# The sign of a float64 weight by a parametric relu on the scalar engine, and a rebuilt order

## The chip, the cores and the metric

The kernel runs on one core of a Trainium2 chip. A core has five engines that run side by side and wait for each other by semaphores: TensorE (PE in the rows; PEld is its weight load), VectorE (DVE), ScalarE (ACT), GpSimd (POOL) and SyncE (SP), which issues the transfers here. The metric is device time in microseconds (us). Each run is one launch of the whole program.

## The reference, cut to what matters

An attention over packed keys feeds two pairs of layers.

```python
p_packed = sm_attn(p, k, v)                 # 8 batches, 8 heads, 576 keys, 32 packed rows
x = sm_attn(q, p_packed, p_packed)          # 4608 tokens x 512
h = x @ w_in                                # 512 -> 2048
P = a[0] + a[1]*h + a[2]*h**2 + a[3]*h**3
Q = 1.0 + abs(b[0])*abs(h) + abs(b[1])*h**2
x = (P / (Q + 1e-06)) @ w_out               # 2048 -> 512
h = x @ w2_in
out = (h - tanh(h)) @ w2_out                # the second pair, same sizes
```

The four weight matrices (`w_in`, `w_out`, `w2_in`, `w2_out`) arrive as float64, everything else as float32. The kernel reads each float64 as a pair of 32-bit words, and the core itself makes float32 values of them.

## The kernel before, in words

The 4608 tokens are cut into ten column blocks n of 384 or 512 tokens (`XW`). A chunk g = 8 n + p is one block and one of eight pieces p of the 2048 hidden columns. For each chunk PE runs `l1` (L610, 12 products per piece of a block, into a two-deep PSUM ring `h`), ACT, POOL and DVE make the rational function, and PE runs `l2` (L623), 16 products with the high part `gh` and 8 with the low part `gl`, into four accumulators. High and low parts together give float32 products out of a faster format, so each layer has three products for one. Six DVE instructions belong to a chunk: L648 and L652 (`front_2`, `front_3`, which read `h`), then L665, L667, L671 and L674 (`back`); L665 writes `gh`, L674 writes `gl`. POOL has one, L645; ACT has five (L633, L637, L641, L657, L658).

Ahead of a block stand a softmax over the packed rows (L502 to L546, on DVE and ACT; L517, L531 and L546 may go to POOL instead) and, for each batch, the packed attention (scores L398, exponent L414, transposes L428, values L443) and a product of `pp` with the first weight (L475), split into high and low by ACT L484 and DVE L488 into `slot`. So the second matrix of the attention is folded into `w_in`.

The second pair follows the 80 chunks: nine blocks of 512 tokens, in each 16 steps of `l3` (L736, 12 products), tanh (ACT L742), subtraction (DVE L745), split into high (ACT L750) and low (DVE L753) and `l4` (L766 to L768, 12 products).

**Float64 weights.** They come as 33 pieces of up to 1 MB into the tile `raw`, of which there are two (`RAW = 2`); a third piece waits until the first is done with. A piece has two words for each number. The class `Weights` makes float32 of them in place:

- step "1" on DVE: L309 shifts the low word right by 29 bits. L312 then takes the sign bit of the high word (and) and puts it on the low word (or).
- step "A" on ACT: L320 multiplies the high word, read as float32, by 2^-112.
- step "2" on DVE: L325 shifts that left by 3 bits and joins it (or) with the low word.

The planner has these as `d1`, `dA` and `d`, each waiting for the one ahead of it. For the weights of `l2`, `l3` and `l4` there follow ACT L933 (high part) and DVE or POOL L937 (low part); the eight pieces of `l1`'s weight go to `w`, which L475 reads, and are stored back to memory for the later batches. Sixteen pieces (`w1`, `w2`) are needed by the first block, the other 17 by the second pair.

**Order.** The class `Plan` sets each engine's order when the program is built: a list of work with costs, `after` lists and due times; at each turn the engine that can start soonest takes the due-first work among what can start within its `SLACK`. The due times are offsets in the table `DUE`. Each engine then runs its instructions in this order, and one that waits holds all behind it. A work marked `port=True` also keeps POOL and DVE apart: POOL's next work waits for the DVE work that stands ahead of it.

Of the kernel before, what the change touches and what calls it, by code (L numbers as in the profile page):

```python
# [12 lines left out]
AF = mybir.ActivationFunctionType  # L13
ALU = mybir.AluOpType
# [3 lines left out]
LN2 = 0.6931471805599453  # L18


DUE = {"G0": 15.294, "G1": -3.281, "A2": 4.445, "P_W": -1.767, "P_F": -15.98, "P_R": -8.628, "P_B": -2.149, "P_2": 3.709, "P_3": 4.233, "P_E": 4.677, "P_4": 7.085, "D_Y": 1.328, "b0": 3.208, "b1": -2.115, "b2": -0.452, "b3": 0.917, "l2h": 2.411, "l2l": 0.922, "f2": -18.573, "f3": -3.699, "fu": 2.695, "ft": 11.608, "fq": -4.098, "gH": -21.109, "gL": -7.224, "mx": -4.057, "ex": 1.371, "z": -6.028, "et": -3.273, "ta": 2.123, "av": -1.372, "y": 4.265, "bt": -27.441, "bd": 5.818, "si": -12.623, "sx": -14.679, "ss": 8.057, "se": -16.289, "sz": 2.679, "sn": 8.64, "so": 7.528, "sh": 11.803, "sl": 7.641, "w1": 1.591, "w2": -1.036, "w3": 7.691, "wh": 5.275, "wl": 2.512, "x": 5.311, "u2": -4.84, "u3": 7.277, "u4": -3.765, "u5": -4.641, "uu0": -3.053, "uu1": -1.728, "r0": -4.745, "dA": 26.416, "wd": -6.518, "d": 1.166}

SLACK = {"ALT": 0, "DVE": 0, "PE": 0.0, "ACT": 97.8, "POOL": 830.6, "SP": 0}


class Plan:
# [11 lines left out]
    ALT = 600  # L38
# [8 lines left out]
    def add(self, name, engine, cost, run, after=(), due=0.0, take=None, free=(), behind=(), late=None, port=None):  # L47

        assert name not in self.work, name
        port = "POOL" in engine if port is None and engine else port
        self.work[name] = [engine, cost, run, list(after), due, take, list(free), list(behind), late, port]
# [116 lines left out]
def packed_attention_moe_kernel(  # L170
# [27 lines left out]
    act, dve, pool, pe, sp = nc.scalar, nc.vector, nc.gpsimd, nc.tensor, nc.sync  # L198
# [32 lines left out]
    def cut(t, n, c=2):  # L231

        return t[:, 0:c * XW[n]].rearrange("p (c t) -> p c t", c=c)
    G0, G1, A2, P_W, P_F, P_R, P_B, P_2, P_3, P_E, P_4, D_Y = (
        DUE[x] for x in "G0 G1 A2 P_W P_F P_R P_B P_2 P_3 P_E P_4 D_Y".split()
    )

    def O(x):
        return DUE.get(x, 0.0)

# [33 lines left out]
    b0, b1 = cabs[:, 0:1], cabs[:, 1:2]  # L274
# [5 lines left out]
    class Weights:  # L280
# [24 lines left out]
        def step(self, j, step, dst=None):  # L305
            w = self.words(j, U32) if wide else None
            if step == "1":

                dve.tensor_scalar(  # L309
                    out=w[:, :, 0], in0=w[:, :, 0], scalar1=29, scalar2=None, op0=ALU.logical_shift_right  # L310
                )
                dve.scalar_tensor_tensor(  # L312
                    out=w[:, :, 0], in0=w[:, :, 1], scalar=0x80000000, in1=w[:, :, 0],
                    op0=ALU.bitwise_and, op1=ALU.bitwise_or,
                )
            if step == "A":


                f = self.words(j)
                act.activation(out=f[:, :, 1], in_=f[:, :, 1], func=AF.Copy, scale=2.0 ** -112)  # L320
            if step == "2":
                def like(x):
                    return x if dst is None else x.rearrange("p (a f) -> p a f", a=4)

                dve.scalar_tensor_tensor(  # L325
                    out=w[:, :, 0] if dst is None else dst.bitcast(U32),
                    in0=like(w[:, :, 1]), scalar=3, in1=like(w[:, :, 0]),
                    op0=ALU.logical_shift_left, op1=ALU.bitwise_or,
                )
            if step == "copy":  # L330
                pool.tensor_copy(out=dst, in_=self.got[j][0].rearrange("p (a f) -> p a f", a=4))
# [13 lines left out]
    sx = ctx.enter_context(ExitStack())  # L345
# [5 lines left out]
    bd, pp = {}, {}  # L351
# [439 lines left out]
    add = plan.add  # L791

    def c_act(n, pointers=0, sbuf=0):
        return 0.833 * n + 52 + 93 * pointers + 43 * sbuf

    def c_dve(n):
        return 1.04 * n + 70
# [64 lines left out]
    for j, (kind, i) in enumerate(pairs):  # L862
        if kind == "w1":
            srcs = w1_parts(i)
            due, free = i - 3.0 + O("w1"), []
            if i % 2 == 0 and i >= 2 * WB:
                gone = (i - 2 * WB, i - 2 * WB + 1)
                free = [("g", 0, x) for x in gone] + ([("w1d", x) for x in gone] if wide and B > 1 else [])
        else:
            if kind == "w2":  # L870
                srcs, slots_, due, free = [w2[2 * i], w2[2 * i + 1]], w2_slot[2 * i:2 * i + 2], i + 0.8 + O("w2"), []
            elif kind == "w3":
                srcs, slots_, due = [w3[i], w3[i + 1]], w3_slot[i:i + 2], total - 16 + 4 * i + O("w3")
            else:
                srcs, slots_, due = [w4[i]], [(w4_slot, i)], total + i - D_Y
                if i + PRE < NF:
                    srcs.append(w3[i + PRE])
                    slots_.append(w3_slot[i + PRE])
            if kind != "w2":
                free = []  # L880
                for x in slots_:
                    if not isinstance(x, tuple):
                        free += last_use(x)
                    elif x[1] < len(w4_slot):
                        free += last_use(x[0][x[1]])
                    else:
                        free += [("open y",)]

            def slots_now(slots_=slots_):
                return [x[0][x[1]] if isinstance(x, tuple) else x for x in slots_]  # L890

        k = len(srcs)
        w1s = kind == "w1"
        if w1s:
            names = [("w1", 0, i)]
        else:
            names = {"w2": [("w2", 2 * i), ("w2", 2 * i + 1)], "w3": [("w3", i), ("w3", i + 1)],
                     "w43": [("w4", i), ("w3", i + PRE)][:k]}[kind]
        if j == NX:
            add_extra()  # L900
        old = raw_free()
        for c, src in enumerate(srcs):
            dma(("raw", j, c), 512 * 128 * (8 if wide else 4), lambda j=j, c=c, src=src: weights.load(j, c, src),
                old, due - 1.5 + O("r0") * (j < 8), behind=raw_next(("raw", j, c)))
        raw_user.append(list(names))
        loads = [("raw", j, c) for c in range(k)]

        def step(x, j=j, w1s=w1s, i=i):
            if w1s and x in ("2", "copy"):
                if i % 2 == 0:  # L910
                    w1_tile(0, i // 2)
                w1_kept[i] = half(w1_t[0, i // 2], i)
                weights.step(j, x, half(w1_t[0, i // 2], i))
            else:
                weights.step(j, x)

        if wide:
            add(("d1", j), "DVE", 90 + k * 800, lambda f=step: f("1"), loads, due, port=True)
            add(("dA", j), "ACT", c_act(512 * k, 0, 1), lambda f=step: f("A"), [("d1", j)], due + O("dA"))
            add(("d", j), "DVE", c_dve(512 * k), lambda f=step: f("2"), [("dA", j)] + (free if w1s else []), due + O("d"), port=True)  # L920
        elif w1s:
            add(("d", j), "POOL", k * 1900, lambda f=step: f("copy"), loads + free, due)
        else:
            add(("d", j), None, 0, lambda: None, loads, due)
        if w1s:
            plan.alias(("w1", 0, i), ("d", j))
            if wide and B > 1:
                dma(("w1d", i), 128 * 4096, lambda i=i: sp.dma_start(out=half(w1d[i // 2], i), in_=w1_kept.pop(i)), [("d", j)], due + 1 + O("wd"))
        else:
            for c in range(k):  # L930
                def high(c=c, j=j, get=slots_now):
                    h, l = halves(get()[c])
                    act.activation(out=h, in_=weights.pieces(j)[c], func=AF.Copy)  # L933

                def low(by, c=c, j=j, get=slots_now):
                    h, l = halves(get()[c])
                    by.tensor_tensor(out=l, in0=weights.pieces(j)[c], in1=h.bitcast(F32), op=ALU.subtract)  # L937

                add(("wh", j, c), "ACT", c_act(512, 0, 1), high, [("d", j)] + free, due + 0.2 + O("wh"))
                add(names[c], ("POOL", "DVE"), (c_low(512), c_dve(512)), low, [("wh", j, c)], due + 0.3 + O("wl"))  # L940
# [19 lines left out]
    for u in range(2 * B):  # L960
        b, d = u // 2, UNIT(u)
# [32 lines left out]
    for b in range(B):  # L994
        for p in range(NP):
            d = p - 2.0 if b == 0 else blocks_of(b)[0] * NP + p - G0
            i = b * NP + p
            k = 2 if b else 1
            if p % k == 0:
# [6 lines left out]
                for y in range(k):  # L1006
                    if i + y >= NG:
                        x, y = divmod(i + y - NG, NP)
# [196 lines left out]
```

## Time and profile before

| | |
|---|---|
| device time, median of 3 runs | 1639.33 us (1637.66 to 1640.53) |
| profiled execution, device time | 1636.56 us |
| its span, first to last instruction | 1634.6 us |
| mean granted TensorE clock | 0.975 |
| busy: PE, DVE, ACT, POOL | 1550.9, 1032.2, 784.7, 180.9 us |
| instructions: PE, DVE, ACT, POOL | 8784, 1193, 1062, 90 |

The span is read in stages, since the mean over it mixes them: the first 200 us, in which 16 weight pieces, the attention and the first chunks share the engines; the chunks up to about 830 us; and the second pair to the end. PE's busy time is that of matmuls that overlap each other, so a busy PE can still run below its best rate; how many matmuls it starts, and how far apart, tells the rest.

### The profile page before, as it was taken

What the parts mean: (1) busy time and instruction counts of PE and PEld (TensorE: products, weight loads), DVE (VectorE), ACT (ScalarE), POOL (GpSimd) and SP (SyncE); (2) the same over time, 40 slices, a digit from 0 to 9 for tenths busy, and PEclk for the clock granted to TensorE, in tenths of its full rate; (3) what the DMA queues carried; (4) which work ended last, traced back from release to release, by engine and by line L of the source; (5) the groups of instructions that cost most, each with busy time, mean ns of one, the idle gap of its engine ahead of it and who ended that gap; (6) DMA issues with size and microseconds to landing.
All of it is one profiled execution on the core that took longest, in us unless ns stands there. A gap on an engine that the chain in (4) does not pass through costs nothing.

```text
span 1634.6 us, 21117 instructions
## 1 busy us (share of the span) xinstructions
PE 1550.9 (95%) x8784; PEld 1267.1 (78%) x8784; DVE 1032.2 (63%) x1193; ACT 784.7 (48%) x1062; POOL 180.9 (11%) x90
## 2 busy tenths in 40 slices
PE   5777999999999999998889999999999999999999
PEld 3556787878888777887877788888888888888887
DVE  4999989988889999999898423232323222232222
ACT  3766666667676676767565322222222222222222
POOL 0102232222121222222200000000000000000000
PEclk7798999999999999999999999999999999999999
DMA  7674122232421212222144200000000001000000
GB/s 280 214 241 175 71 78 103 82 128 81 143 87 57 98 68 98 93 97 90 52 148 155 78 1 26 27 26 26 26 26 27 26 13 39 0 20 20 0 27 26
DMA packets 46127, 125.69 MB, mean 77 GB/s; under 512 B 4432, under 2 KB 14800, under 8 KB 42448
## 3 DMA queue, kind: packets, MB, share of 16 engines
q1 hardware_dynamic: 46032, 124.34, 21.8%
q8 instruction: 69, 1.13, 0.3%
q14 instruction: 26, 0.21, 0.0%
HBM read 101.26 MB, written 23.07 MB: 76 GB/s over the span
## 4 chain that ended last, share of the span: by engine, by line
PE 75%; DVE 13%; ACT 7%; issue 3%; POOL 1%; DMA 1%; SPq 0%; DVEq 0%; ACTq 0%; POOLq 0%
PE h L736 24%; PE acc L623 17%; PE h L610 9%; PE acc L767 7%; PE acc L766 7%; PE acc L768 7%; PE h L475 2%; DVE m L667 2%; DVE raw L312 1%; DVE m L671 1%; ACT t L633 1%; DVE gh L665 1%; DVE t L648 1%; POOL m L645 1%; DVE raw L309 1%
## 5 line engine op out<-in xcount | busy, mean ns | idle before, releaser
L736 PE MATMUL h<-xh,slot 128*128 128x512 f32 x1152 | 388.0, 398 | 6.7 <-DVE t L745 5.1
L753 DVE TENSOR_TENSOR yl<-t,yh 128x512 fp32r<-128x512 f32 x144 | 99.7, 692 | 365.5 <-ACT yh L750 365.5
L750 ACT ACTIVATE yh<-t 128x512 fp32r<-128x512 f32 x144 | 91.0, 632 | 369.3 <-PE acc L768 368.3
L736 PEld LDWEIGHTS h<-xh,slot 128*128 128x128 f32 x1152 | 217.3, 189 | 63.2 <-DVE t L745 9.5
L736 PE MATMUL h<-xl,slot 128*128 128x512 f32 x576 | 229.1, 398 | 0.0
L610 PE MATMUL h<-ah,slot 128*128 128x320 f32 (+3 forms) x1024 | 217.2, 306 | 0.0
L623 PE MATMUL acc<-gh,slot 128*128 128x512 f32 (+1 forms) x800 | 182.3, 382 | 10.5 <-DVE slot L937 6.3
L645 POOL TENSOR_TENSOR m<-u,r 128x1024 f32<-128x1024 f32 (+1 forms) x60 | 129.5, 2158 | 487.2 <-ACT r L641 195.7
L623 PEld LDWEIGHTS acc<-gh,slot 128*128 128x128 f32 x800 | 152.3, 199 | 37.3 <-DVE slot L937 7.7
L610 PEld LDWEIGHTS h<-ah,slot 128*128 128x128 f32 x1024 | 172.5, 195 | 1.5
L623 PE MATMUL acc<-raw,slot 128*128 128x512 f32 (+1 forms) x720 | 166.4, 380 | 0.0
L610 PE MATMUL h<-al,slot 128*128 128x192 f32 (+3 forms) x512 | 152.2, 310 | 9.2 <-DVE t L652 4.9
L745 DVE TENSOR_TENSOR t<-h,t 128x512 f32<-128x512 f32 x144 | 99.4, 691 | 90.2 <-ACT t L742 84.6
L623 PEld LDWEIGHTS acc<-raw,slot 128*128 128x128 f32 x720 | 130.2, 188 | 30.0 <-issue 8.4
L767 PE MATMUL acc<-slot,yh 128*128 128x512 f32 x360 | 140.9, 391 | 0.0
L766 PE MATMUL acc<-slot,yl 128*128 128x512 f32 x360 | 140.7, 391 | 0.0
L768 PE MATMUL acc<-slot,yh 128*128 128x512 f32 x360 | 140.0, 389 | 0.0
L742 ACT ACTIVATE t<-h 128x512 f32<-128x512 f32 x144 | 85.9, 597 | 104.5 <-DVE yl L753 90.1
L736 PEld LDWEIGHTS h<-xl,slot 128*128 128x128 f32 x576 | 108.8, 189 | 25.1
L610 PEld LDWEIGHTS h<-al,slot 128*128 128x128 f32 x512 | 99.2, 194 | 19.4 <-issue 6.8
L637 ACT ACTIVATE u<-h 128x1024 f32<-128x1024 f32 (+1 forms) x80 | 74.4, 930 | 60.4 <-PE h L610 60.2
L623 PE MATMUL acc<-gl,slot 128*128 128x384 f32 (+1 forms) x400 | 94.7, 379 | 8.4 <-DVE gl L674 8.4
(94 smaller groups left out, 2301.8 us busy)
## 6 DMA issues: line engine op xcount, KB each, us to landing
raw<-in_w_dram SPq DMA_DIRECT2D x64, 512.0 KB, 4.6
w<-w1d SPq DMA_DIRECT2D x28, 1024.0 KB, 4.8
k<-in_kT_dram SPq DMA_DIRECT2D x16, 576.0 KB, 4.0
xr<-x2d SPq DMA_DIRECT2D x36, 256.0 KB, 2.7
out_dram<-raw SPq DMA_DIRECT2D x36, 256.0 KB, 2.0
v<-in_va_dram SPq DMA_DIRECT2D x16, 512.0 KB, 5.2
q<-in_qT_dram SPq DMA_DIRECT2D x6, 1024.0 KB, 5.6
x2d<-q SPq DMA_DIRECT2D x12, 512.0 KB, 3.0
```

The lines of the kernel that those rows point to most:

```text
L610: pe.matmul(out=ps[:, f, t], lhsT=x, rhs=y, start=(i == 0), stop=(i == len(seq) - 1))
L623: pe.matmul(out=acc_t[n][m][:, 0:XW[n]], lhsT=w2_slot[2 * p + f][:, o:o + 128], rhs=x[:, f, :], start=(p == 0 and part == 512 and f == 0), ...
L637: act.activation(out=u_t[g], in_=hv(g), func=AF.Abs)
L645: pool.tensor_tensor(out=q_m[g], in0=u_t.pop(g), in1=r_t[g], op=ALU.mult)
L736: pe.matmul(out=hy(i, f), lhsT=a, rhs=b, start=(j == 0), stop=(j == len(seq) - 1))
L742: act.activation(out=th_t[i, f][:, 0:w], in_=hy(i, f), func=AF.Tanh)
L745: dve.tensor_tensor(out=t, in0=hy(i, f), in1=t, op=ALU.subtract)
L750: act.activation(out=yh_t[i, f][:, 0:w], in_=t, func=AF.Copy)
L753: dve.tensor_tensor(out=yl_t[i, f][:, 0:w], in0=t, in1=yh_t[i, f][:, 0:w].bitcast(F32), op=ALU.subtract)
L766: pe.matmul(out=a, lhsT=gl[:, c], rhs=s[:, 0:512], start=(f == 0), stop=False)
L767: pe.matmul(out=a, lhsT=gh[:, c], rhs=s[:, 512:1024], start=False, stop=False)
L768: pe.matmul(out=a, lhsT=gh[:, c], rhs=s[:, 0:512], start=False, stop=(f == NF - 1))
```

## The change

DVE's L312 goes. The sign comes from ACT: the multiplication by 2^-112 is done by a parametric relu whose slope for negative values is 2^32, so that a negative number is multiplied by 2^-80 in all. Its exponent is then 32 higher than a positive number's would be, and that one bit of the exponent, shifted left by 3 in step "2", lands on the place of the sign. The number of instructions on ACT is the same. Since the low word no longer needs the high word's sign, `dA` waits for the load alone and may run beside `d1`; `d` waits for both. Planned costs of `d1` are lowered, and the tables `DUE` and `SLACK` hold other numbers, so that the order on all engines is another one.

```diff
-DUE = {"G0": 15.294, "G1": -3.281, "A2": 4.445, ...
-SLACK = {"ALT": 0, "DVE": 0, "PE": 0.0, "ACT": 97.8, "POOL": 830.6, "SP": 0}
+DUE = {"G0": 8.347, "G1": 18.444, "A2": 4.011, ...
+SLACK = {"ALT": 0, "DVE": 0, "PE": 323.5, "ACT": 94.9, "POOL": 488.4, "SP": 0}
...
                 dve.tensor_scalar(
                     out=w[:, :, 0], in0=w[:, :, 0], scalar1=29, scalar2=None, op0=ALU.logical_shift_right
                 )
-                dve.scalar_tensor_tensor(
-                    out=w[:, :, 0], in0=w[:, :, 1], scalar=0x80000000, in1=w[:, :, 0],
-                    op0=ALU.bitwise_and, op1=ALU.bitwise_or,
-                )
             if step == "A":
...
-                act.activation(out=f[:, :, 1], in_=f[:, :, 1], func=AF.Copy, scale=2.0 ** -112)
+                act.activation(out=f[:, :, 1], in_=f[:, :, 1], func=AF.Prelu, scale=2.0 ** -112, alpha=2.0 ** 32)
...
-            add(("d1", j), "DVE", 90 + k * 800, lambda f=step: f("1"), loads, due, port=True)
-            add(("dA", j), "ACT", c_act(512 * k, 0, 1), lambda f=step: f("A"), [("d1", j)], due + O("dA"))
-            add(("d", j), "DVE", c_dve(512 * k), lambda f=step: f("2"), [("dA", j)] + (free if w1s else []), due + O("d"), port=True)
+            add(("d1", j), "DVE", 60 + k * 330, lambda f=step: f("1"), loads, due, port=True)
+            add(("dA", j), "ACT", c_act(512 * k, 0, 1), lambda f=step: f("A"), loads, due + O("dA"))
+            add(("d", j), "DVE", c_dve(512 * k), lambda f=step: f("2"), [("d1", j), ("dA", j)] + (free if w1s else []), due + O("d"), port=True)
```

From L312 on, lines of the changed program have numbers that are three lower (L325 becomes L322, L320 becomes L317, L937 becomes L934, and so on).

DVE's order at the third and fourth weight pieces of the first block, before:

```order
L309 TENSOR_SCALAR raw_325<-raw_325 128x1024
L312 SCALAR_TENSOR_TENSOR raw_325<-raw_325 128x1024
L648 TENSOR_TENSOR t0_249<-t0_249,h_388 128x768
L652 SCALAR_TENSOR_TENSOR t0_249<-t0_249,coa_92,h_388 128x768
L648 TENSOR_TENSOR t1_250<-t1_250,h_409 128x768
L309 TENSOR_SCALAR raw_404<-raw_404 128x1024
L312 SCALAR_TENSOR_TENSOR raw_404<-raw_404 128x1024
L325 SCALAR_TENSOR_TENSOR w1_439<-raw_325 128x4x256
L652 SCALAR_TENSOR_TENSOR t1_250<-t1_250,coa_92,h_409 128x768
L665 SCALAR_TENSOR_TENSOR gh0_257<-t0_249,coa_92,r0_253 128x768
L325 SCALAR_TENSOR_TENSOR w1_439<-raw_404 128x4x256
```

The same place in the changed program:

```order
L309 TENSOR_SCALAR raw_319<-raw_319 128x1024
L322 SCALAR_TENSOR_TENSOR w1_388<-raw_319 128x4x256
L645 TENSOR_TENSOR t0_247<-t0_247,h_356 128x768
L649 SCALAR_TENSOR_TENSOR t0_247<-t0_247,coa_92,h_356 128x768
L645 TENSOR_TENSOR t1_248<-t1_248,h_374 128x768
L309 TENSOR_SCALAR raw_369<-raw_369 128x1024
L322 SCALAR_TENSOR_TENSOR w1_388<-raw_369 128x4x256
L662 SCALAR_TENSOR_TENSOR gh0_255<-t0_247,coa_92,r0_251 128x768
```

Two L312 are gone, and the joining step stands right behind the shift of its own piece, where it used to stand behind work of a chunk.

DVE's order at the end of the chunks, just ahead of the second pair's first subtraction (L745), before:

```order
L671 SCALAR_TENSOR_TENSOR m1_256<-t1_250,coa_92,m1_256 128x768
L325 SCALAR_TENSOR_TENSOR raw_6665<-raw_6665 128x1024
L674 TENSOR_TENSOR gl0_258<-m1_256,r1_254 128x768
L937 TENSOR_TENSOR slot24_89<-raw_6635,slot24_89 128x512
L937 TENSOR_TENSOR slot8_73<-raw_6635,slot8_73 128x512
L937 TENSOR_TENSOR slot25_90<-raw_6665,slot25_90 128x512
L937 TENSOR_TENSOR slot9_74<-raw_6665,slot9_74 128x512
L745 TENSOR_TENSOR t_6824<-h_6639,t_6824 128x512
```

In the changed program:

```order
L309 TENSOR_SCALAR raw_6750<-raw_6750 128x1024
L671 TENSOR_TENSOR gl0_256<-m1_254,r1_252 128x768
L934 TENSOR_TENSOR slot16_81<-raw_6714,slot16_81 128x512
L322 SCALAR_TENSOR_TENSOR raw_6750<-raw_6750 128x1024
L934 TENSOR_TENSOR slot11_76<-raw_6750,slot11_76 128x512
L934 TENSOR_TENSOR slot17_82<-raw_6750,slot17_82 128x512
L742 TENSOR_TENSOR t_6823<-h_6612,t_6823 128x512
```

In the changed program two further pieces (raw_6714 and raw_6750) are made ahead of the first subtraction, which stood behind it before.

ACT's order at the first two weight pieces and the first softmax, before:

```order
L521 ACTIVATE q<-q 128x768
L320 ACTIVATE raw<-raw 128x1024 x2
L414 ACTIVATE k,z<-h,mx 128x576
L484 ACTIVATE slot_81<-h 128x512
L541 ACTIVATE ah<-q 128x768
```

In the changed program:

```order
L317 ACTIVATE raw<-raw 128x1024
L518 ACTIVATE q<-q 128x768
L317 ACTIVATE raw<-raw 128x1024
L481 ACTIVATE slot_81<-h 128x512
L538 ACTIVATE ah<-q 128x768
```

The first piece's multiplication stands ahead of the softmax's exponent now, as it has no step of DVE ahead of it.

Four of ten L531 (128x1024, softmax times reciprocal) go from DVE to POOL, three of 36 L715 (the second pair's input, low part) as well; one L546 comes from POOL to DVE. ACT has one table load at the start and one at the first tanh, before and after.

## Rows read from the trace of the kernel before

**Rows 1.** Windows by stage: start:end, length, busy us (count) by engine, clock, DMA, GB/s.

```profile
core 0: us, PE busy (x) PEld busy (x) DVE busy (x) ACT busy (x) POOL busy (x), PEclk, DMA share, GB/s
0.00:20.00 20.00, 10.21 (x146) 4.76 (x146) 5.11 (x12) 6.04 (x16) 0.34 (x6) 1.00 0.90 327
20.00:155.00 135.00, 94.62 (x854) 73.19 (x854) 124.22 (x157) 85.95 (x129) 14.65 (x8) 0.80 0.64 219
155.00:200.00 45.00, 40.15 (x268) 34.69 (x269) 41.48 (x39) 30.16 (x34) 14.53 (x7) 0.96 0.24 88
200.00:700.00 500.00, 492.04 (x3459) 407.72 (x3458) 458.51 (x467) 345.70 (x413) 123.27 (x55) 0.99 0.27 93
700.00:835.00 135.00, 121.47 (x653) 106.25 (x651) 125.89 (x127) 87.49 (x103) 28.09 (x14) 0.97 0.21 72
835.00:910.00 75.00, 72.30 (x301) 57.63 (x302) 68.85 (x94) 45.69 (x69) 0.00 (x0) 0.96 0.49 169
910.00:1634.60 724.60, 720.08 (x3109) 582.88 (x3107) 208.17 (x304) 183.66 (x302) 0.00 (x0) 1.00 0.07 23
```

**Rows 2.** Chain that ended last, 210 to 220 us: start, length, what.

```profile
212.49 3.10 PE h L610 x24
215.59 3.65 PE acc L623 x16
```

**Rows 3.** Windows of L312 alone: start:end, length, DVE busy (count), clock, DMA, GB/s.

```profile
20.00:155.00 135.00, 19.65 (x16) 0.80 0.64 219
...
700.00:835.00 135.00, 6.13 (x5) 0.97 0.21 72
835.00:910.00 75.00, 13.65 (x12) 0.96 0.49 169
```

**Rows 4.** Groups by line: form xcount | busy us, mean ns | idle ahead, releaser.

```profile
L312 DVE SCALAR_TENSOR_TENSOR raw<-raw 128x1024 uint32<-128x1024 uint32 (+1 forms) x33 | 39.4, 1195 | 1.1
L320 ACT ACTIVATE raw<-raw 128x1024 f32<-128x1024 f32 (+1 forms) x33 | 37.1, 1126 | 19.1 <-DVE raw L312 17.5 <-ACT pp L468 1.0
L309 DVE TENSOR_SCALAR raw<-raw 128x1024 uint32<-128x1024 uint32 (+1 forms) x33 | 22.2, 673 | 3.8 <-DMA raw<-in_w_dram 3.6
L633 ACT ACTIVATE t<-h,coa 128x1024 f32<-128x1024 f32 (+1 forms) x80 | 89.3, 1118 | 26.5 <-PE h L610 22.2 <-DVE m L671 4.0
```

**Rows 5.** Waits of PE, then of DVE, 20 to 155 us: who, total, times, longest.

```profile
PE h L475 <- DVE w L325: 10.8, 2, 5.7
PE acc L623 <- DVE slot L937: 6.3, 4, 3.0
...
DVE t L648 <- ACT t L633: 4.4, 2, 3.2
DVE raw L309 <- DMA raw<-in_w_dram: 1.9, 2, 1.6
```

**Rows 6.** Waits of PE, 700 to 835 us, and its longest of 835 to 910 us.

```profile
PE acc L623 <- DVE gl L674: 4.3, 2, 3.0
PE acc L623 <- DVE gh L665: 4.2, 2, 3.3
...
PE h L736 <- DVE t L745: 5.1, 2, 4.9
```

**Rows 7.** Groups by line: L531 and L715 on DVE, and L546 on POOL.

```profile
L531 DVE TENSOR_TENSOR q<-q,ssum 128x1024 f32<-128x1024 f32 (+1 forms) x10 | 11.3, 1131 | 0.0
L715 DVE TENSOR_TENSOR xl<-xr,xh 128x512 fp32r<-128x512 f32 x36 | 24.1, 687 | 4.1 <-ACT xh L710 3.6
L546 POOL TENSOR_TENSOR al<-q,ah 128x1024 fp32r<-128x1024 f32 x1 | 2.4, 2417 | 4.5 <-ACT ah L541 4.5
```

**Rows 8.** Timeline of POOL, then of DVE: start us, length us, instruction.

```profile
747.42 2.38 POOL L645 TENSOR_TENSOR m<-u,r 128x1024 f32<-128x1024 f32 x1 [4.83 <-ACT r L641]
...
747.72 3.16 DVE L667 SCALAR_TENSOR_TENSOR m<-m,gh 128x1024 f32<-128x1024 f32 x1
755.20 1.22 DVE L667 SCALAR_TENSOR_TENSOR m<-m,gh 128x1024 f32<-128x1024 f32 x1
```

**Rows 9.** Groups by line: the table loads of ACT.

```profile
L1152 ACT ACT_TABLE_LOAD x1 | 1.3, 1283 | 0.7 <-PEq L1194 0.7
L742 ACT ACT_TABLE_LOAD x1 | 1.3, 1283 | 0.0
```

**Rows 10.** L674, first to last start: count, ns least/median/most, us.

```profile
L674 DVE TENSOR_TENSOR gl<-m,r x40: 942/1036/1764, 55.9 to 828.9; 128x768 fp32r<-128x768 f32 x21, 128x1024 fp32r<-128x1024 f32 x19
```

More of the change, by code (lines that the diff above doesn't have):

```diff
@@ L18 @@
 LN2 = 0.6931471805599453
-DUE = {"G0": 15.294, "G1": -3.281, "A2": 4.445, "P_W": -1.767, "P_F": -15.98, "P_R": -8.628, "P_B": -2.149, "P_2": 3.709, "P_3": 4.233, "P_E": 4.677, "P_4": 7.085, "D_Y": 1.328, "b0": 3.208, "b1": -2.115, "b2": -0.452, "b3": 0.917, "l2h": 2.411, "l2l": 0.922, "f2": -18.573, "f3": -3.699, "fu": 2.695, "ft": 11.608, "fq": -4.098, "gH": -21.109, "gL": -7.224, "mx": -4.057, "ex": 1.371, "z": -6.028, "et": -3.273, "ta": 2.123, "av": -1.372, "y": 4.265, "bt": -27.441, "bd": 5.818, "si": -12.623, "sx": -14.679, "ss": 8.057, "se": -16.289, "sz": 2.679, "sn": 8.64, "so": 7.528, "sh": 11.803, "sl": 7.641, "w1": 1.591, "w2": -1.036, "w3": 7.691, "wh": 5.275, "wl": 2.512, "x": 5.311, "u2": -4.84, "u3": 7.277, "u4": -3.765, "u5": -4.641, "uu0": -3.053, "uu1": -1.728, "r0": -4.745, "dA": 26.416, "wd": -6.518, "d": 1.166}
-SLACK = {"ALT": 0, "DVE": 0, "PE": 0.0, "ACT": 97.8, "POOL": 830.6, "SP": 0}
+DUE = {"G0": 8.347, "G1": 18.444, "A2": 4.011, "P_W": 0.635, "P_F": -18.129, "P_R": -4.378, "P_B": -6.522, "P_2": 2.576, "P_3": -1.6, "P_E": 8.199, "P_4": 0.069, "D_Y": -0.884, "b0": 6.443, "b1": 0.529, "b2": 5.78, "b3": 3.656, "l2h": 26.183, "l2l": -0.554, "f2": -19.364, "f3": -3.463, "fu": 9.473, "ft": 18.383, "fq": -20.432, "gH": -14.269, "gL": -11.53, "mx": -21.824, "ex": -28.042, "z": -4.847, "et": -6.32, "ta": 16.84, "av": -4.076, "y": -7.188, "bt": -35.685, "bd": 15.515, "si": -32.287, "sx": -4.66, "ss": -1.47, "se": -25.833, "sz": 18.591, "sn": 12.907, "so": 24.305, "sh": 29.06, "sl": -8.673, "w1": 3.17, "w2": -1.834, "w3": 0.833, "wh": 6.617, "wl": 1.919, "x": 10.912, "u2": -4.978, "u3": 20.333, "u4": -2.188, "u5": -10.126, "uu0": -3.106, "uu1": -4.482, "r0": -6.673, "dA": 34.131, "wd": -12.354, "d": 4.032}
+SLACK = {"ALT": 0, "DVE": 0, "PE": 323.5, "ACT": 94.9, "POOL": 488.4, "SP": 0}
 class Plan:
```

## The prediction

> **What bounds the kernel now.** I read the windows by stage first, since the mean busy share of DVE (63% of the span) belongs to no stage. [rows 1] falls into four parts.
>
> From 910 us on, PE is busy 720.08 of 724.60 us and starts 3109 matmuls, one in 232 ns. DVE has 208 of 725 us to do. Nothing that DVE is spared there moves the end.
>
> From 200 to 700 us both engines are nearly full: PE 492.04 of 500 us, DVE 458.51. Which of them paces is told by PE's rate: in the chain of waits 16 matmuls of `l2` take 3.65 us [rows 2], 228 ns each, as close together as in the last stage. So PE runs at its best there, and DVE, 92% busy, keeps up with some 41 us to spare.
>
> From 20 to 155 us it is the other way. DVE is busy 124.22 of 135 us, PE 94.62, at a mean clock of 0.80, so that PE's part also holds time at the 1.2 GHz level. What PE waits for is DVE: 10.8 us for the joining step L325, 6.3 us for L937 [rows 5]. Transfers are little waited for: DVE's waits for a weight piece are 1.9 us.
>
> From 700 to 835 us DVE paces again, more mildly: 125.89 of 135 us, PE 121.47, with waits for L674 and L665 [rows 6].
>
> **The change, part by part.** The sum is made against the profiled execution, 1636.56 us, of which 1634.6 us are the span. The median of the runs shown, 1639.33 us, is 2.8 us above it; the difference that I work out is taken off the median.
>
> *L312 goes.* It is 33 instructions, 39.4 us, 1195 ns each [rows 4]. What counts is where they lie [rows 3]: 16 with 19.65 us from 20 to 155 us, 5 with 6.13 us from 700 to 835 us, 12 with 13.65 us from 835 to 910 us.
>
> *The first stage.* DVE's list there is shorter by 19.65 us and has nothing new in it: up to the 13th L674, the order of before and that of after differ by the 16 L312 and by three instructions that after does earlier (one L937, one L546, one L536), which are not extra work. Two bounds. At least 8 us: the shorter stage must move the same bytes, and what DVE no longer does, it may wait for pieces or for ACT instead. Against much of that speaks that 219 GB/s over 135 us would become 256 GB/s over 115 us, under the 327 GB/s of the first 20 us [rows 1]. At most 24 us: beside its own work DVE may lose its waits for ACT (4.4 us, [rows 5]), since the ACT multiplication no longer stands behind L309 and L312, and L325 with it comes some 1.9 us sooner after its load (673 and 1195 ns, [rows 4]). I take 19 us, near the row, because DVE has so little idle time in this stage that work removed from it can hardly turn into waiting: 135 less 124.22 is 10.8 us in all. A warmer PE is not counted.
>
> *The multiplication on ACT as a parametric relu.* No row has this function. On 128x1024 the plain multiplication takes 1126 ns and the dearer form with two operands per partition 1118 ns [rows 4]. Bounds: nothing, or half as much again (0.6 us for each, 16 times, 9 us), on an engine that is busy 85.95 of 135 us. ACT's idle time hides either. I take nothing. What stands behind it on DVE is the joining step, which now follows its own shift closely in the order; if ACT is late, DVE waits with all that is queued behind, chunks' steps above all. That is part of the 8 us bound.
>
> *The table.* [rows 9] show what a change of ACT's function table costs, 1283 ns, and that there are two in the whole run. The order of after has two as well, at the same places. A function that isn't in the table at hand would need more: that is a rival below.
>
> *The middle, 200 to 700 us.* Four L531 go to POOL; on DVE they cost 1131 ns each [rows 7], so its list is 4.5 us shorter. PE paces, so this gives nothing by itself. DVE enters the stage with its lead, and PE's idle time (8 us) may shrink; the order is a new one and may also make it grow. Bounds: 6 us of gain to 10 us of loss; I take 2 us of gain, since DVE's spare time in the stage becomes larger, not smaller.
>
> On POOL the nearest row for such a tensor by tensor is 2417 ns [rows 7], and POOL holds DVE up at times: an L667 that starts 0.3 us after POOL's L645 takes 3.16 us, another of its form 1.22 us [rows 8]. The Trainium skill (SBUF — State Buffer, section Terms) says that DVE and GpSimd arbitrate for one pair of ports, that the pair is locked for a whole instruction, and that the loser stands still. The trace agrees: 1.94 us of standing still within POOL's 2.38 us. By that rule the four moved L531 could cost DVE up to 4 x 2.4 us less the 4.5 us saved, 5 us of loss; in a stage that PE paces the sum stays as it is.
>
> *The last chunks, 700 to 835 us.* Five L312 go there (6.13 us), and two L715 of 687 ns go to POOL ahead of the first L745 [rows 7]. But the order shows what comes in their place: two more weight pieces stand ahead of the first subtraction of the second pair, with L309, two L325 and four L937. Counted from the 69th L674 to the first L745 and priced by the rows, DVE has the same 83 us of work in both. So the stage gets shorter only as far as PE's waits go (4.3 and 4.2 us, and 5.1 us just after, [rows 6]). Bounds: nothing, and all of PE's idle time there, 13.5 us. I take 4 us.
>
> *From 835 us on.* The 12 other L312 lie beside a PE that is busy 72.30 of 75 us [rows 1]: nothing.
>
> **Sum**: 19 + 2 + 4 = 25 us less. The profiled execution would take 1611.6 us, the median 1639.33 - 25 = **1614 us**.
>
> **Rivals.**
>
> *1. The waits vanish altogether.* DVE is 25 us ahead, and PE, once it has work, loses almost none: 19.65 + 6 + 13.5 = 39 us, **1600 us**. For it: the total work taken off DVE in these stages is about that. Against: the last stage's work on DVE is the same.
>
> *2. The first stage has another pace.* If the two `raw` tiles, with the load of each 1 MB piece, set how often a piece comes, a spared L312 gives only its part of a tile's round, and the stage gives 8 us, the others 2: **1629 us**. For it: DMA's share is 0.64 there, the highest after the start. Against: DVE waits 1.9 us for pieces.
>
> *3. More table loads.* The Trainium skill (ScalarE: Activation LUTs, section Table sets: the hidden batching unit) says that functions are loaded in named sets, and that a function outside the set at hand needs a load. As a mechanism here, from rows: each of the 33 multiplications would bring two loads of 1283 ns, in the first stage 16 x 2.57 = 41 us on top of ACT's 86, so 127 us, 11 more than the 116 that DVE would need; the end would be some 11 us later than in the sum: **1625 us**. Against: the order of after has two loads. The Trainium skill (ScalarE: Activation LUTs, section What ACT_TABLE_LOAD costs) gives 2.66 us for a change with its drain; with that figure, an estimate, ACT would need 171 us in the stage, and the kernel would be slower.
>
> *4. The order of the middle is worse: slower.* In 700 to 835 us, with DVE late, PE's idle share is 10.0% (13.5 of 135), in 200 to 700 us 1.6%. If the new order, which lets PE take work up to 323.5 ns ahead of what is due and puts softmax work on POOL ahead of chunks, brings the middle to the idle share of the later stage, that costs 8.4% of 500 us, 42 us, against 19 in front and none behind: 23 us more, **1662 us**. The point from which it decides is 25 us of new idle time of PE between 200 and 835 us. Against: DVE has less to do in the middle than before.
>
> **How the numbers follow.** My forecast, 1614 us, 62%. Rival 1 10%, rival 2 13%, rival 3 3%, rival 4 8%, and 4% that it all comes to nothing, a first-stage gain that the middle gives back. Faster by over 0.2% (3.3 us, about what a measurement of this kernel can tell from no change): 88%. Within 0.2%: 4%. Slower: 8%. The range takes in the bounds of the terms: 24 + 6 + 13.5 us of gain give 1596, rival 2 with a little of the middle's loss 1633.
>
> **What would show it.** L312's group is gone and DVE's total is down by about 40 us. The multiplication's mean stays near 1126 ns, with two table loads. L674's last start, at 828.9 us now [rows 10], comes about 25 us earlier, and from there to the end the time is what it was, some 806 us. The first stage carries most of it: PE's idle time up to 200 us is 9.8 + 40.4 + 4.9 = 55 us now [rows 1] and should be some 35. The forecast is wrong if PE's idle time from 200 to 700 us is well over 10 us, if the multiplication takes over 2 us, or if DVE's waits for weight pieces or for ACT in the first stage come to over 10 us.

## The result, and the profile after

The changed kernel takes **1618.28 us** (median of 4 runs, 1618.05 to 1619.01), the kernel before 1639.34 (4 runs). The ratio is 0.9873, 95% interval 0.9856 to 0.9890: 21 us faster, where 25 were forecast. Its profiled execution took 1618.31 us, of which the span is 1616.4, at a mean clock of 0.981. The profile of the kernel before is of an execution of 1636.56 us, 2.8 us under that kernel's median, so the two profiles show 18.2 of the 21 us.

The windows by stage, in the columns of [rows 1]:

```profile
0.00:20.00 20.00, 11.80 (x146) 5.95 (x146) 3.36 (x10) 7.06 (x17) 0.34 (x6) 1.00 0.87 302
20.00:155.00 135.00, 101.57 (x886) 81.95 (x887) 118.70 (x153) 94.23 (x136) 20.75 (x11) 0.85 0.67 227
155.00:200.00 45.00, 45.00 (x332) 36.66 (x331) 42.16 (x43) 28.28 (x34) 11.50 (x5) 1.00 0.29 100
200.00:700.00 500.00, 492.72 (x3471) 406.88 (x3470) 460.10 (x468) 349.54 (x417) 127.87 (x58) 1.00 0.27 95
700.00:835.00 135.00, 118.08 (x596) 104.41 (x596) 121.83 (x132) 92.28 (x115) 28.86 (x16) 0.94 0.29 101
835.00:910.00 75.00, 74.87 (x325) 60.60 (x324) 42.45 (x62) 34.07 (x53) 0.00 (x0) 1.00 0.34 117
```

PE's idle time, stage length less busy time, tells where the time went. Up to 200 us it was 55.1 us [rows 1] and is 8.2 + 33.4 + 0 = 41.6. From 200 to 700 us it was 8.0 and is 7.3. From 700 to 910 us it was 13.5 + 2.7 = 16.2 and is 16.9 + 0.1 = 17.0. So the idle time saved lies in the first stage. Over the whole span it went from 83.7 to 69.9 us, 13.8 less. The span is 18.2 us shorter; the other 4.4 us are PE's own busy time (the first lines of both pages: 1550.9 us before, 1546.5 now). The granted clock of 20 to 155 us rose from 0.80 to 0.85, which goes with it; no run changes the clock alone.

```profile
PE 1546.5 (96%) x8784; PEld 1265.9 (78%) x8784; DVE 987.4 (61%) x1155; ACT 781.7 (48%) x1062; POOL 189.3 (12%) x95
```

The groups that answer to [rows 4, 7, 9], line first, then count, busy us and mean ns:

```profile
L317 ACT ACTIVATE raw<-raw 128x1024 f32<-128x1024 f32 (+1 forms) x33 | 37.4, 1135 | 8.1 <-DMA raw<-in_w_dram 8.0
L528 POOL TENSOR_TENSOR q<-q,ssum 128x1024 f32<-128x1024 f32 x4 | 7.7, 1920 | 23.7 <-DVE m L664 13.3 <-ACT slot L481 7.7 <-DVE ssum L524 2.8
L1149 ACT ACT_TABLE_LOAD x1 | 1.3, 1283 | 0.7 <-PEq L1191 0.7
L739 ACT ACT_TABLE_LOAD x1 | 1.3, 1283 | 0.0
```

The parametric relu takes 1135 ns where the multiplication took 1126 (33 times 9 ns, 0.3 us in all). What L317 waits for is its transfer, no longer DVE's L312. There are two table loads, as before.

Waits of 20 to 155 us that answer to [rows 5] (total, times, longest), PE's first:

```profile
PE h L472 <- DVE w L322: 6.7, 2, 5.2
...
PE acc L620 <- DVE slot L934: 3.6, 2, 3.1
```

```profile
DVE t L645 <- ACT t L630: 4.0, 5, 1.4
DVE raw L309 <- DMA raw<-in_w_dram: 2.5, 1, 2.5
DVE w L322 <- ACT raw L317: 2.4, 2, 1.9
```

PE waits 6.8 us less for DVE's weights (10.8 + 6.3 before). DVE's waits for a weight piece or for ACT were 1.9 + 7.0 us and come to some 10 in all.

L671, the old L674 of [rows 10]:

```profile
L671 DVE TENSOR_TENSOR gl<-m,r x40: 939/1070/2003, 51.4 to 813.0; 128x768 fp32r<-128x768 f32 x21, 128x1024 fp32r<-128x1024 f32 x19
```

The last of the chunks' `gl` starts at 813.0 us, 15.9 us earlier. From there to the end of the span it took 805.7 us and takes 803.4.

PE's waits from 700 to 835 us have not shrunk as [rows 6] would:

```profile
PE h L733 <- DVE t L742: 6.5, 1, 6.5
PE acc L620 <- DVE gh L662: 4.7, 3, 2.8
PE h L607 <- DVE t L649: 3.6, 1, 3.6
PE acc L620 <- DVE gl L671: 2.1, 1, 2.1
```

The longest is the passage from the chunks to the second pair, where it was 4.9 us. The timeline there shows its chain (start us, length us, instruction, idle time ahead and who ended it):

```profile
812.99 0.95 DVE L671 TENSOR_TENSOR gl<-m,r 128x768 fp32r<-128x768 f32 x1
...
814.00 1.78 PE L620 MATMUL acc<-gl,slot 128*128 128x384 f32 x8 [2.05 <-DVE gl L671]
...
815.77 1.23 ACT L930 ACTIVATE slot<-raw 128x512 fp32r<-128x512 f32 x2 [2.66 <-PE acc L620]
...
816.89 1.62 ACT L681 ACTIVATE q<-acc 128x384 f32<-128x384 f32 x4
...
818.53 1.28 ACT L739 ACT_TABLE_LOAD   x1
...
819.83 1.08 ACT L739 ACTIVATE t<-h 128x512 f32<-128x512 f32 x2
...
820.94 1.29 DVE L742 TENSOR_TENSOR t<-h,t 128x512 f32<-128x512 f32 x2 [3.18 <-ACT t L739]
...
822.29 0.79 PE L733 MATMUL h<-xh,slot 128*128 128x512 f32 x1 [6.51 <-DVE t L742]
```

ACT does two weight copies, four spills of the accumulators, the table load and two tanh, one behind the other; then comes DVE's subtraction. PE stands for 6.5 us. In the kernel before, the copies nearest to the passage ended ahead of the last `l2`, and ACT waited for that before its spills:

```profile
829.03 1.24 ACT L933 ACTIVATE slot<-raw 128x512 fp32r<-128x512 f32 x2 [0.81 <-DVE raw L325]
...
831.20 1.64 ACT L684 ACTIVATE q<-acc 128x384 f32<-128x384 f32 x4 [0.93 <-PE acc L623]
```

### The profile page after: what moved, and what is told of

Read it like the earlier page. It is cut to its first block, busy times and chain, and to the rows that moved or that the text cites. A ratio compares the mean times of both kernels' runs of the same rounds, so it can differ in the third digit from the quotient of the medians.

```text
span 1616.4 us, 21317 instructions
## 1 busy us (share of the span) xinstructions
PE 1546.5 (96%) x8784; PEld 1265.9 (78%) x8784; DVE 987.4 (61%) x1155; ACT 781.7 (48%) x1062; POOL 189.3 (12%) x95
## 5 line engine op out<-in xcount | busy, mean ns | idle before, releaser
L750 DVE TENSOR_TENSOR yl<-t,yh 128x512 fp32r<-128x512 f32 x144 | 99.4, 691 | 84.2 <-ACT yh L747 83.2
L654 ACT ACTIVATE r<-m,lnb 128x1024 f32<-128x1024 f32 (+1 forms) x60 | 63.5, 1058 | 74.3 <-POOL m L642 74.1
L645 DVE TENSOR_TENSOR t<-t,h 128x1024 f32<-128x1024 f32 (+1 forms) x80 | 88.5, 1106 | 16.1 <-ACT t L630 16.0
```

The lines of the kernel that those rows point to most:

```text
L645: dve.tensor_tensor(out=t_t[g], in0=t_t[g], in1=hv(g), op=ALU.mult)
L750: dve.tensor_tensor(out=yl_t[i, f][:, 0:w], in0=t, in1=yh_t[i, f][:, 0:w].bitcast(F32), op=ALU.subtract)
```

## The experiments

The theory behind the prediction: VectorE paces the first stage, so L312's time there is the gain, and the relu costs nothing. The rivals: the gain comes from the new order; the loads pace the first stage; the relu has a hidden price; the last 17 pieces count too. "Old sign" is L312 together with the plain multiplication. Line numbers of the experiments differ by a few from those above. The last two columns are from one profile each: start of the last `gl` of the chunks, and span from there to the end.

| run | median us (range) | ratio to before, 95% | last `gl` | rest |
|---|---|---|---|---|
| before | 1639.3 (1637.7 to 1640.5) | | 828.9 | 805.7 |
| after | 1618.28 (1618.05 to 1619.01) | 0.9856 to 0.9890 | 813.0 | 803.4 |
| e1: relu, old order | 1622.73 (1621.85 to 1623.64) | 0.9882 to 0.9915 | 815.1 | 804.7 |
| e2: old sign, new order | 1655.37 (1654.05 to 1656.64) | 1.0081 to 1.0111 | 837.5 | 817.3 |
| e3: new order, old sign in pieces 1 to 16 | 1633.52 (1632.80 to 1634.75) | 0.9949 to 0.9975 | 827.8 | 805.0 |
| e4: new order, old sign in the last 17 | 1641.04 (1639.83 to 1643.63) | 1.0000 to 1.0018 | 822.6 | 816.2 |
| e5: old order, relu in pieces 1 to 16 | 1626.25 (1626.07 to 1632.05) | 0.9910 to 0.9950 | | |
| e6: after, shift cut short in 1 to 16 | 1613.98 (1610.30 to 1615.63) | 0.9826 to 0.9861 | 809.4 | 803.6 |
| e7: after, shift cut short in the last 17 | 1616.81 (1616.27 to 1617.64) | 0.9848 to 0.9881 | 811.4 | 803.5 |
| e8: after, table load ahead of the spills | 1618.96 (1616.55 to 1620.38) | 0.9853 to 0.9886 | 815.2 | 803.2 |
| e9: after, plain copy for the relu | 1620.46 (1617.97 to 1621.11) | 0.9866 to 0.9895 | 815.2 | 803.7 |
| e10: after, one more DVE step in the last 17 | 1638.37 (1637.52 to 1640.29) | 0.9986 to 1.0004 | 822.5 | 815.0 |
| e11: after, table load behind the last exponential | 1617.55 (1616.60 to 1618.89) | 0.9849 to 0.9881 | 814.4 | 801.7 |
| e12: e11, two copies later | 1620.11 (1617.92 to 1620.22) | 0.9863 to 0.9898 | 813.7 | 802.3 |

The profile of e5 is of its longest run, 1632.05 us, while the other three took 1626.07 to 1626.31, so its median alone is used.

### The relu or the order: e1 and e2

e1 keeps the tables, costs and waits of the kernel before and changes the sign alone:

```diff
-                dve.scalar_tensor_tensor(
-                    out=w[:, :, 0], in0=w[:, :, 1], scalar=0x80000000, in1=w[:, :, 0],
-                    op0=ALU.bitwise_and, op1=ALU.bitwise_or,
-                )
...
-                act.activation(out=f[:, :, 1], in_=f[:, :, 1], func=AF.Copy, scale=2.0 ** -112)
+                act.activation(out=f[:, :, 1], in_=f[:, :, 1], func=AF.Prelu, scale=2.0 ** -112, alpha=2.0 ** 32)
```

> The order, planned costs and dependences of before; only the parametric relu in and L312 out. Theory A (the 16 L312 of the first stage were on the path, the new order is worth little): 1620 to 1626 us. Rival B (the new order brings the gain): 1633 us or more.

Measured: 17 us less than before. e2 is the reverse: it undoes these lines in the changed kernel and keeps the new order.

> The order of after, with L312 put back behind L309 and the plain multiplication instead of the relu, for all 33 pieces. Theory A: 1634 to 1642 us, the time of before. Rival B: 1626 us or less, since the order would do without the removal.

Measured: 15 to 16 us **more** than before, outside what either theory had said. So the order is no gain by itself. With the relu in it is worth 4.4 us (1622.73 to 1618.28; the runs don't overlap), with the old sign it costs 15. The windows of e2 show where, in the columns of [rows 1]:

```profile
200.00:700.00 500.00, 492.79 (x3487) 406.92 (x3486) 462.12 (x471) 350.37 (x418) 130.74 (x59) 1.00 0.26 92
...
835.00:910.00 75.00, 58.47 (x221) 45.46 (x220) 60.60 (x81) 40.30 (x62) 1.31 (x1) 0.87 0.44 151
```

The middle is undisturbed. From 835 to 910 us PE idles 16.5 us, against 2.7 before.

e1's first stage, window and DVE's longest wait, shows the other thing:

```profile
20.00:155.00 135.00, 99.36 (x912) 77.03 (x912) 113.67 (x150) 92.99 (x138) 19.65 (x11) 0.86 0.66 228
```

```profile
DVE t L644 <- ACT t L629: 10.2, 5, 4.3
```

DVE's idle time there went from 10.8 us to 21.3: part of what was removed came back as waiting for ACT (4.4 us in [rows 5], 10.2 now). And the clock is 0.86 against 0.80.

### Which pieces count: e3, e4 and e5

```diff
+                if j < 16:          # e3; e4: j >= 16
+                    dve.scalar_tensor_tensor(
+                        out=w[:, :, 0], in0=w[:, :, 1], scalar=0x80000000, in1=w[:, :, 0],
+                        op0=ALU.bitwise_and, op1=ALU.bitwise_or,
+                    )
```

and the plain multiplication for the same pieces. e5 is e1 with the old sign left in pieces 17 to 33.

> The order of after; L312 and the plain multiplication for the first 16 pieces only. Theory A: 1632 to 1638 us, nearly all the gain lost again. Rival C (a spared DVE instruction is worth the same wherever it stands, so half the gain hangs on either half): 1627 to 1630 us.

> The order of after; L312 and the plain multiplication for the last 17 pieces only (w3, w4). Theory A: 1618 to 1621 us, the 17 lie beside a full PE or behind the wait for the first tanh. Rival D (the last chunks do get shorter by L312's absence there, and the new order hides it): 1623 to 1627 us, about 6 us more than after.

> The order of before; the relu and no L312 in the first 16 pieces, L312 and the plain multiplication in the last 17. The whole of the relu in this order gave 17.4 us (1622.7). Theory A (the first stage carries it): 1624 to 1627 us. Rival (the last 17 carry half, as they do in the order of after): 1629 to 1632 us.

| | pieces 1 to 16 | the last 17 |
|---|---|---|
| worth of the relu in the old order | 1639.6 - 1626.25 = 13.4 us | 1626.25 - 1622.73 = 3.5 us |
| worth of it in the new order | 1633.52 - 1618.28 = 15.2 us | 1641.04 - 1618.28 = 22.8 us |

The runs of a row were not all made together. Taken each against the runs of the kernel before that were made with it, the four differences are 13.4, 4.0, 14.5 and 22.0 us.

e3 and e5 came out as the theory said. e4 did not: L312 in the last 17 pieces, which the prediction held for nearly free, costs in the new order more than its whole time (17 L312 are 19.8 us there). The waits of PE in e4 from 822 to 900 us:

```profile
PE h L741 <- DVE t L750: 11.2, 3, 5.5
PE acc L771 <- DVE yl L758: 2.5, 1, 2.5
PE acc L628 <- DVE gl L679: 2.1, 1, 2.1
```

and DVE's timeline just behind the passage:

```profile
831.78 0.69 DVE L309 TENSOR_SCALAR raw<-raw 128x1024 uint32<-128x1024 uint32 x1
832.50 1.23 DVE L313 SCALAR_TENSOR_TENSOR raw<-raw 128x1024 uint32<-128x1024 uint32 x1
833.65 1.29 DVE L758 TENSOR_TENSOR yl<-t,yh 128x512 fp32r<-128x512 f32 x2
834.85 0.69 DVE L720 TENSOR_TENSOR xl<-xr,xh 128x512 fp32r<-128x512 f32 x1
835.46 1.22 DVE L330 SCALAR_TENSOR_TENSOR raw<-raw 128x1024 uint32<-128x1024 uint32 x1
836.59 1.28 DVE L750 TENSOR_TENSOR t<-h,t 128x512 f32<-128x512 f32 x2
```

DVE runs without a gap, and the subtraction L750 that PE waits for stands behind the steps of a weight piece, L313 (the old L312) among them. Of e4's 22.4 us of span, 9.6 lie ahead of the last `gl` and 12.8 behind it. In the old order 12 of these L312 lay beside a full PE [rows 1, 3] and were worth 3.5 us with the other five; in the new one the pieces come earlier (the last L309 starts at 866.9 us in the changed kernel, at 906.5 before), among the last chunks and the first steps of the second pair, where DVE has little slack: in the changed kernel it is busy 37.33 of the 42 us from 821 to 863.

### DVE's time or the chain of a piece: e10

In e4 a piece has one more step on DVE and its ACT step waits for it. e10 leaves the relu and gives the last 17 pieces an idle step of L312's form on the low word alone, for which ACT doesn't wait:

```diff
+                if j >= 16:
+                    dve.scalar_tensor_tensor(
+                        out=w[:, :, 0], in0=w[:, :, 0], scalar=0, in1=w[:, :, 0],
+                        op0=ALU.bitwise_and, op1=ALU.bitwise_or,
+                    )
```

> The kernel after, with one more DVE instruction of L312's form behind L309 in the last 17 pieces, which joins the low word with itself and does not touch the high word, so that ACT's multiplication doesn't wait for it. Theory (DVE's time alone makes the 23 us): 1637 to 1642 us. Rival (the chain of one piece, with the multiplication behind L312, makes a good part of it): 1625 to 1633 us.

The kernel takes 1638.37 us. The 17 steps are 19.8 us of DVE, and the kernel takes 20.1 us longer: microsecond for microsecond, so DVE's time alone explains it. That leaves 2.7 us of e4 for the longer chain of a piece, which is about as much as the runs of e4 and of e10 scatter (3.8 and 2.8 us).

### Is there more of the kind: e6 and e7

The shift L309 works on 8 of 1024 columns, for pieces 1 to 16 (e6) or 17 to 33 (e7), and the join reads the high word twice; so the low words' bits are left out of these weights.

```diff
+                n = 8 if j < 16 else w.shape[1]     # e7: j >= 16
-                    out=w[:, :, 0], in0=w[:, :, 0], scalar1=29, ...
+                    out=w[:, 0:n, 0], in0=w[:, 0:n, 0], scalar1=29, ...
...
-                    in0=like(w[:, :, 1]), scalar=3, in1=like(w[:, :, 0]),
+                    in0=like(w[:, :, 1]), scalar=3, in1=like(w[:, :, 1 if j < 16 else 0]),
```

> The kernel after, with L309 cut to 8 of its 1024 columns in the first 16 pieces and the joining step reading the high word twice, so the low bits of these weights are left out: 16 x 0.6 = 10 us less on DVE in the first stage. Theory (DVE still paces the first stage): 1608 to 1611 us. Rival (loads, ACT or PE pace it now): 1614 us or more.

> The kernel after, with the same cut of L309 in the last 17 pieces (low bits of those weights left out): 17 x 0.6 = 10 us less on DVE at the end of the chunks and just after. Theory (DVE paces the passage to the second pair, as the 23 us of the run with the old sign in the last 17 say): 1610 to 1614 us. Rival (the passage in the kernel after is held by the wait for the first tanh, not by DVE's work): 1617 us or more.

The cut takes 8.4 us off the shifts of either half (11.0 to 2.6 us in e6, 11.2 to 2.8 in e7), less than the 10 expected. In the first stage that gives 4.3 us, 1613.98, practically what the rival of e6 had; the four runs of e6 lie 5.3 us apart, so the size is rough. Off the last 17 pieces it gives 1.5, 1616.81, a little under what the rival of e7 had. DVE paces the first stage of the changed kernel only in part now. At the end the worth of DVE's time breaks off: 20 us more cost 20, 8.4 us less give 1.5. That the passage stands on ACT's chain fits this, for PE's longest wait of e7 there is the one of after:

```profile
PE h L734 <- DVE t L743: 6.6, 1, 6.6
```

### The price of the relu: e9

```diff
-                act.activation(out=f[:, :, 1], in_=f[:, :, 1], func=AF.Prelu, scale=2.0 ** -112, alpha=2.0 ** 32)
+                act.activation(out=f[:, :, 1], in_=f[:, :, 1], func=AF.Copy, scale=2.0 ** -112)
```

> The changed kernel with the scaling of a weight piece as a plain copy with a scale in place of the parametric relu (the sign of a weight is left out of the result). Theory A, the relu costs ScalarE no more than the multiplication that it replaced (1135 ns against 1126 ns, and the table loads are the same two): within 1 us of the changed kernel, 1617 to 1619.5 us. Rival B, the relu's slope brings a cost that the durations don't show (a table held or fetched, a longer start): 1612 to 1616 us.

1620.46 us, a little over the forecast interval and certainly not faster, with the same two table loads and 1132 ns for one copy: the relu hides no cost.

### The passage: e8, e11 and e12

```diff
     def spill(n, i):
+        if n == NB - 1 and i == 0:                               # e8
+            act.preload_act_table_set("exp_and_others")
...
         act.activation(out=r, in_=r, func=AF.Exp, scale=-1.0, bias=lnb[:, 1:2])
+        if g == NB * NP - 1:                                     # e11, e12
+            act.preload_act_table_set("exp_and_others")
```

> The changed kernel with one instruction more: ScalarE loads the table of exp and tanh just ahead of the four spills of the last block, while it waits for that block's l2, and not behind them, ahead of the first tanh. In the profile of the changed kernel the passage from the last l2 to the next h keeps PE waiting 6.5 us for t, whose chain is spills, table load (1283 ns), tanh, VectorE's t. Theory A, this chain holds the passage: the load's 1.28 us come off, 1616.5 to 1617.5 us against 1618.3, and PE's longest wait there falls to about 5.2 us. Rival B, PE or VectorE is late there for another reason, or the chip loads the table again where it did before: 1618 to 1619 us.

e8 saved nothing, as its rival had it, and ACT's timeline says why:

```profile
818.02 1.23 ACT L932 ACTIVATE slot<-raw 128x512 fp32r<-128x512 f32 x2 [2.55 <-DVE raw L322]
...
819.28 1.28 ACT L679 ACT_TABLE_LOAD   x1
820.57 1.64 ACT L683 ACTIVATE q<-acc 128x384 f32<-128x384 f32 x4
```

The copies L932 wait for DVE's join and end after the last `l2` does; load and spills then stand in one row as before, only the other way round.

> The changed kernel with ScalarE's second table load (for tanh) put right behind the last exponential, some 9 us ahead of the passage, where ScalarE has idle time (1.35 and 2.66 us ahead of two weight copies), and not ahead of the first tanh. The load put just ahead of the spills, in the run before this, saved nothing: ScalarE was still held by the copies of a weight piece when the last l2 ended, and load and spills then stood in one row as before. Theory A, ScalarE's row of copies, load, spills and tanh holds the passage: with the load out of the row PE's wait for t falls from 6.5 to about 5.2 us and the time by 1.3 us, 1616.5 to 1617.5 us. Rival B, something else holds the passage: PE's wait stays at 6.5 us, 1618 to 1619 us.

> The kernel with the load behind the last exponential, and besides the two copies and two subtractions of the last weight piece ahead of the spills (ScalarE's L930, VectorE's L934) put behind the first pair of tanh steps. Theory A: ScalarE's row at the passage loses the load's 1.28 us and about 1.1 us of copies, so PE's wait for t falls from 6.5 to about 4.1 us, and the time by 2.4 us, 1615 to 1616.5 us. Rival B, PE's wait is set elsewhere or the delayed weights are waited for later: 1617 to 1619 us.

e11 takes 1617.55 us. It does shorten that wait, by more than forecast: to 3.95 us. But a wait ahead of it grew. DVE's timeline ahead of the passage, then PE's, in e11:

```profile
810.19 1.23 DVE L322 SCALAR_TENSOR_TENSOR raw<-raw 128x1024 uint32<-128x1024 uint32 x1 [1.44 <-ACT raw L317]
...
815.37 2.93 PE L620 MATMUL acc<-gl,slot 128*128 128x384 f32 x8 [3.49 <-DVE gl L673]
...
822.25 0.79 PE L735 MATMUL h<-xh,slot 128*128 128x512 f32 x1 [3.95 <-DVE t L744]
```

The load now delays the relu of a weight piece, DVE's join waits 1.44 us for it, and with it the last `gl`, for which PE waits 3.49 us instead of 2.05. The eight products behind that wait take 2.93 us instead of 1.78. The two waits and the products between them come to 10.37 us in e11 and 10.34 in the changed kernel, so nothing is gained up to the first `l3`. The time is 0.7 us under the changed kernel, within the scatter of both. In e12 the two weight copies on ACT come later too. There the copies' two subtractions on DVE stayed in their places, ahead of the copies, so the low parts of those two weight pieces are not what they should be. The wait for t falls to 3.07 us, but the time is 1620.11: not as forecast. The profile is of the shortest of the four runs, 1617.92 us, while the other three took 1620.08 to 1620.22, so it can't show what they lost. In it PE is busy 73.64 of 75 us from 835 to 910, where it was 74.87: two further waits for t, 0.91 and 0.45 us. What took the rest back stays open. None of the three beats the changed kernel by more than the runs scatter: the last `gl` alone differs by 2.2 us between profiles of after, e8 and e9, whose programs are the same in the chunks but for e9's copy.

## Why the prediction was right, and where its steps were off

**The first stage** was put at 19 us and is worth 13.4 (e5) to 15.2 (e3). The mechanism held: VectorE paced, and the gain is its shorter list. That it is VectorE's time, and not the shorter chain of a piece, was run apart only for the last 17 pieces (e10). For the first 16 it is read from a row: in the kernel before, the join into `w` waited for ACT's multiplication only 0.4 us from 20 to 155 us:

```profile
DVE w L325 <- ACT raw L320: 0.4, 1, 0.4
```

The size was off because the step read 10.8 us of idle time as proof that removed work could hardly turn into waiting. It did: in e1 DVE's idle time doubled and its waits for ACT with it, and e6 shows that a further 8.4 us there give 4.3. The lower bound's argument was the right one, for ACT rather than for the loads.

**"A warmer PE is not counted."** It should have been: 4.4 of the span's 18.2 us are PE's busy time. What of it falls into the first stage is inside the 13.4 to 15.2 us, though, and no term beside them.

**The total** came within 4 us by some luck. The runs split it as 13.4 us for the first 16 pieces (e5), 3.5 for the last 17 in the old order (e1 against e5) and 4.4 for the new order (after against e1), 21.3 in all. The sum had 19 for the first, nothing for the 12 of the last 17 that lie beyond 835 us, and 2 + 4 for gains in the middle and in the last chunks that PE's idle time there hardly shows. What the first stage gave less was made up in part by gains that the sum had at other places.

**The relu at nothing**: right (1135 against 1126 ns, two loads, e9). The rival with more table loads (3) fell. The Trainium skill (ScalarE: Activation LUTs, section Table sets: the hidden batching unit), by which a function outside the set at hand brings a load, is not contradicted: no load appeared beside the relu, so here it cost none in either of the two sets.

**The middle**, 2 us of gain: PE's idle time fell by 0.7 us. PE paces there, as the step said. The four softmax products on POOL took 1920 ns each, under the 2417 ns taken from [rows 7]; of the 5 us that the prediction worked out from the rule of the Trainium skill (SBUF — State Buffer, section Terms) nothing is to be seen in PE's idle time. Nor is it in DVE's: what ran beside the four products took no longer than its like elsewhere, an L645 on 128x1024 1.21 us here and 1.21 in the median. One of the four:

```profile
192.68 1.21 DVE L645 TENSOR_TENSOR t<-t,h 128x1024 f32<-128x1024 f32 x1
192.90 1.92 POOL L528 TENSOR_TENSOR q<-q,ssum 128x1024 f32<-128x1024 f32 x1 [6.64 <-DVE m L664]
193.80 0.68 DVE L485 TENSOR_TENSOR slot<-h,slot 128x512 fp32r<-128x512 f32 x1
```

So the standing still of [rows 8] does not come with every pair of instructions on the two engines.

**The last chunks**, 4 us of gain: wrong, it is nothing. PE's idle time of 700 to 910 us went from 16.2 to 17.0 us. The step had counted well that DVE has the same work there in both orders (by the two traces 90.3 and 91.4 us from the 69th L674 to the first subtraction, where it priced 83), and still let PE's waits shrink. They didn't. Of the 17.0 us, 10.4 are waits for the chunks' `gh`, `t` and `gl`, which DVE still makes with a list as long as before. The other 6.5 are the passage, which stands on ACT's chain of copies, spills, load and tanh; it was 4.9 us before and is 4.9 in e1, so its growth comes with the new order.

**From 835 us on**, nothing: right for the old order, in which these L312 lay beside a full PE (3.5 us for all 17 in e5 against e1). But the step priced them by the old order's place. In the new one the pieces have moved to where DVE paces, and the same 17 would cost 22.8 us (e4). The relu pays for that move, and the step did not see it.

**Rivals 1 and 2** fell. Of PE's 83.7 us of idle time 69.9 are left, so its waits did not vanish. The loads do not pace the first stage: VectorE waits 2.5 us for a piece there, 1.9 before.

**Rival 4**, a worse order, named the wrong place: the middle is undisturbed. The mechanism exists, at the passage, and decides when the old sign is back (e2, 15 us slower than before). The rival also read PE's slack the wrong way round: 323.5 lets PE stand that many ns for work that is due sooner; it doesn't let PE take work ahead.

**The marks**: the last `gl` came 15.9 us earlier, not 25; the rest took 803.4 us, where some 806 were forecast; PE's idle time up to 200 us is 41.6, not 35. Of the three signs of a wrong forecast two stayed away, and VectorE's waits for pieces and ACT in the first stage came to some 10 us, at the mark. L312's group is gone and DVE's total 44.8 us lower, 40 forecast.

## What to carry to other kernels

Price a removed instruction at the place that it will have in the new order, not at the one it has in the trace: the same 17 instructions were worth 3.5 us in one order and 22.8 in another. When an engine that paces is relieved, look who is next: a stage with little idle time can still turn removed work into waiting for a second engine, and here it gave back a quarter to a third of the time removed. A part that moves work from a full engine to a free one and a part that rebuilds the order should be run apart, both ways round, for their worths do not add: here the relu alone gave 17 us, the order alone cost 15 to 16, and both together gave 21.

## What the runs showed of the hardware

**Behind waits of one length PE ran at either level of its clock.** Ahead of the last eight `l2` products PE stands for 2.05 us in the changed kernel, 2.08 in e9 and 3.49 in e11. The same eight then take 1.78, 2.91 and 2.93 us. The windows (columns of [rows 1]) of the changed kernel, of e9 and of e11:

```profile
814.00:815.90 1.90, 1.77 (x8) 1.35 (x8) 1.68 (x2) 0.13 (x1) 0.00 (x0) 0.88 0.24 32
```

```profile
816.10:819.10 3.00, 2.91 (x8) 2.40 (x8) 2.20 (x4) 1.15 (x3) 0.00 (x0) 0.52 0.43 130
```

```profile
815.30:818.30 3.00, 2.93 (x8) 2.42 (x8) 2.20 (x4) 1.15 (x3) 0.00 (x0) 0.51 0.47 130
```

The granted clock is 0.88 on the mean in the first, and 0.52 and 0.51, the lower of the two levels (1.2 GHz), in the others; in e8 a wait of 2.04 us is followed by a clock of 1.00 and 1.67 us for the eight. So a wait of 2 us was followed by up to 1.2 us of slower matmuls in one profile and by none in another, and its length alone doesn't tell which. After the passage's 6.51 us in the changed kernel the clock is 0.50 for the next 3 us, in which PE starts 7 products:

```profile
822.20:825.20 3.00, 2.91 (x7) 2.33 (x8) 3.00 (x6) 3.00 (x6) 0.00 (x0) 0.50 0.64 247
```

**A parametric relu on ScalarE costs what a copy costs**: 1135 ns against 1126 in the kernel before and 1132 in e9, on 128x1024 words read and written with a stride of two, with a slope of 2^32 and a scale of 2^-112, and without a table load beside it.
